# When the second mixing's weights are prepared: sums of half groups in blocks 2 to 6, second-layer parts in blocks 7 and 8, both kept in DRAM

## The chip, the core and the metric

The kernel runs on one core of a Trainium2 chip. The metric is the device time of one execution in microseconds (us), of which three runs of the kernel before are given. A core has five engines that work through their own queues in order: TensorE (PE, with its weight loads PEld), VectorE (DVE), ScalarE (ACT), GpSimd (POOL) and SyncE (SP), which here only issues transfers. ACT and POOL issue transfers too.

## The reference, cut to what matters

Three stages follow each other. Everything is float32; the weights come as float64 and are read as pairs of 32-bit words.

```
attention   (8 batches, 8 heads, 576 tokens, 64 wide): softmax of q over the width, of k over the tokens,
            kv = k_s^T v, out = q_s kv
first mixing   u  = x + (relu(x^T w_tok1) w_tok2)^T
               y  = u + relu(u w_ch1) w_ch2              512 -> 1536 -> 512
second mixing  xn = (y - mean) / sqrt(var + 1e-6) * g_ln
               out = y + relu(xn w2_ch1) w2_ch2          512 -> 2048 -> 512
```

## The kernel before, in words

Each float32 operand of a product is split into a high part (rounded by a copy to fp32r) and a low part (the rest), and three of the four partial products are made (`PASSES`). ACT makes the high part, POOL or DVE the low one. A weight in float64 is first turned into float32 bits: ACT rescales the upper word (`rebias`, L113), DVE makes three integer operations (L119, L126, L132), and then the two parts follow.

The first mixing runs over 4608 tokens in blocks of 512 tokens, numbered 0 to 8. A block makes 12 steps f; in each, `L1` makes 12 matmuls into `ph`, ACT and DVE take relu and split it into `h` (L155, L156), and `L2` makes 12 matmuls of the `h` of two steps earlier. In blocks 1 to 6 the attention of the next batch is made between these: a block has four units, and the function `Unit.start` sets on which tick (four ticks to a step) each unit's pieces are emitted. For the change it matters that a unit passes through all engines: DVE takes maxima `kmx`, `qm` and `kmd`, POOL subtracts (`qt` L486, `kt` L501), ACT takes exponentials, DVE sums `qs` (L518 to L520), POOL normalises `qt` (L521) and makes the low part of `qn` (L150, L530), PE multiplies `pk` and `pg`. At step 1 of a block the result of the block before is taken out of PSUM (`finish`: DVE `yT`, L745, then four POOL additions, L748) and turned back by PE (`py`, L659, in `y_store`).

The second mixing multiplies by w2_ch1 with seven products in place of eight for a 2 x 2 split (the sums S1 to S4 of weight quarters and the like sums of activations), over 6 slabs of 768 tokens and 8 groups of weights: 48 turns q, each with seven products `pp` (L1207) and the second layer of the turn before (`token_chunk`, L1245). `gather` on DVE and ACT takes each product out of one of two PSUM banks, so product i+2 waits for the gather of product i.

Before, `combine_all` decodes w2_ch1, makes the sums and splits them during blocks 7 and 8, and stores them in `wc_dram`; the turns load them from there (`ring_load`). The second-layer weights w2_ch2 (16 chunks of 128 rows) are loaded, decoded and split in place by `w2_jobs`: two chunks in block 8, two in turn 0 and twelve in turns 1 to about 6, a few operations after each product (`work`). There they share DVE, ACT and POOL with the gathers, the means and roots of the last block (`Root`, L775 to L789) and the normalisation of the next slab (`hat`, L1088, on POOL).

The order on each engine is the order in which the code emits; nothing reorders it. So an instruction that waits holds up all that stands behind it on its engine.

Of the kernel before, what the change touches and what calls it, by code (L numbers as in the profile page):

```python
# [8 lines left out]
F32 = mybir.dt.float32  # L9
# [15 lines left out]
def kernel(  # L25
# [66 lines left out]
    wc_dram = dram.tile([NP, P, 7, 512], F32, name="wc_dram")  # L92
# [586 lines left out]
    class Phase1:  # L679
# [51 lines left out]
        def finish(self):  # L731
# [9 lines left out]
            yT_t[self.j] = main.tile([P, KD, BLK], F32, tag="y", bufs=1, name="yT")  # L741
            yT, u = yT_t[self.j], u_t[self.j]
            for dd in range(KD):
                x = self.part[dd // 2][:, dd % 2] if self.f0 else u[:, 0, dd].bitcast(F32)
                nc.vector.tensor_tensor(out=yT[:, dd], in0=self.acc[dd], in1=x, op=ALU.add)  # L745
            def add(c):
# [14 lines left out]
    class Root:  # L761
# [5 lines left out]
        def start(self, at):  # L767
            for n, fn in zip((0, 2, 8, 11), (self.root, self.rstd, self.turn, self.store)):
                later(at + n, fn)
# [52 lines left out]
    SUMS = (1, 3, 4, 5)  # L822

    class Combine:


        def __init__(self, g):
            self.g = g

        def load(self):  # L830
            self.st = []
            for i in range(2):
                st = stage(512)
                a = w2_ch1[2 * i * P:2 * (i + 1) * P, 4 * self.g * P:4 * (self.g + 1) * P]
                nc.sync.dma_start(
                    out=st.rearrange("p (k f) t -> p k (f t)", k=2),
                    in_=a.rearrange("(k p) f -> p k f", p=P),
                )
                self.st.append(st)

        def decoding(self):

            both = [decode(st, None, None, None) for st in self.st]
            ops = [b[0] for b in both]
            for b in both:
                ops += [lambda b=b: [b[n]() for n in (1, 2, 3)], nop, nop]
            raw = [
                st[:, :, 0].bitcast(F32).rearrange("p (k f) -> p k f", k=2) for st in self.st
            ]
            self.a = {(f, k): raw[k][:, :, f * P:(f + 1) * P] for f in range(2) for k in range(2)}  # L850
            box = {}

            def add(o, x, y, op):
                def fn():
                    if o == 1:
                        self.s = w2p[0].tile([P, 4, 2, P], F32, tag="xc", bufs=7, name="wsum")
                    s = self.s
                    v = {"S1": s[:, 1], "S2": s[:, 0], "S3": s[:, 2], "S4": s[:, 3]}
                    pick = lambda n: v[n] if n in v else self.a[n]
                    nc.vector.tensor_tensor(out=s[:, o], in0=pick(x), in1=pick(y), op=op)  # L860
                return fn

            A11, A12, A21, A22 = (0, 0), (0, 1), (1, 0), (1, 1)
            ops += [
                add(1, A21, A22, ALU.add), add(0, "S1", A11, ALU.subtract),
                add(2, A11, A21, ALU.subtract), add(3, A12, "S2", ALU.subtract),
            ]
            return ops

        def splitting(self):  # L870
            s, a, box = self.s, self.a, {}
            A11, A12, A22 = a[0, 0], a[0, 1], a[1, 1]
            ops = []

            def tile_of(i):
                n = 0 if i < 3 else 3 if i < 5 else 5
                m = 3 if n == 0 else 2
                if n not in box:
                    box[n] = w2p[0].tile([P, m, 2, 2, P], F32R, tag="xc", bufs=7, name="wc")
                return box[n], i - n  # L880

            def part(x, i, n=1):
                def hi():
                    t, k = tile_of(i)
                    o = t[:, k:k + n, 0] if n > 1 else t[:, k, 0]
                    nc.scalar.activation(out=o, in_=x, func=AF.Copy)

                def lo():
                    t, k = tile_of(i)
                    o, h = (t[:, k:k + n, y] if n > 1 else t[:, k, y] for y in (1, 0))  # L890
                    nc.gpsimd.tensor_tensor(out=o, in0=x, in1=h.bitcast(F32), op=ALU.subtract)  # L891

                return [hi, lo]

            def store(n, m):
                def fn():
                    nc.sync.dma_start(
                        out=wc_dram[self.g, :, n:n + m],
                        in_=box[n].rearrange("p i x k f -> p i (x k f)").bitcast(F32),
                    )  # L900
                return fn

            ops += part(A11, 0) + part(A12, 2) + part(A22, 6)
            ops += part(s[:, 0], 1) + [store(0, 3)]
            ops += part(s[:, 1:3], 3, 2) + [store(3, 2)]
            ops += part(s[:, 3], 5) + [store(5, 2)]
            return ops

    w2p = []
    nop = lambda: None  # L910

    with tc.manual_schedule():
# [75 lines left out]
        jobs = []  # L988

        def work(n):  # L990
            for _ in range(n):
                if jobs:
                    jobs.pop(0)()

        def combine_all():

            cs = [Combine(g) for g in range(NP)]

            def expand(g):

                d = cs[g].decoding() if g < NP else []
                f = cs[g - 1].splitting() if g else []
                if 0 < g < NP - 1:
                    f.insert(6, cs[g + 1].load)
                ops = []
                while f or d[:-4]:
                    if f:
                        ops.append(f.pop(0))
                    if len(d) > 4:
                        ops.append(d.pop(0))  # L1010
                ops += d
                if g < NP:
                    ops.append(lambda: expand(g + 1))
                jobs[0:0] = ops

            jobs.extend([cs[0].load, cs[1].load] + [nop] * 20 + [lambda: expand(0)])

        def w2_jobs(chunks, stages, depth, ts=None, gap=12):

            st = {}  # L1020

            def load(n):
                g, i = n // 2, n % 2
                if i == 0:
                    wb2[g] = main.tile([P, 2, 2, DM], F32R, tag="w", bufs=NF1, name="w")
                st[n] = stages(n)
                nc.sync.dma_start(
                    out=st[n].rearrange("p d t -> p (d t)"), in_=w2_ch2[n * P:(n + 1) * P, :]
                )

            def go(n):
                ops = decode(
                    st[n], lambda x: x, wb2[n // 2][:, 0, n % 2], wb2[n // 2][:, 1, n % 2],
                    ts and ts[n % 2],
                )
                if not ts:
                    ops = [ops[0], lambda x=ops: [x[k]() for k in (1, 2, 3)], nop, ops[4]]
                jobs[0:0] = ops

            out = [lambda n=n: load(n) for n in chunks[:depth]] + [nop] * gap  # L1040
            for k, n in enumerate(chunks):
                out.append(lambda n=n: go(n))
                if k + depth < len(chunks):
                    m = chunks[k + depth]
                    out.append(lambda m=m: load(m))
            return out
# [4 lines left out]
        def ring_tile(i, x):  # L1051
            m = 4 if x == 0 else 3
            ring[i, x] = main.tile([P, m, 2, 2, P], F32R, tag="w", bufs=NF1, name="wr")

        def ring_load(q, x):
            n, m = ((0, 4), (4, 3))[x]
            nc.sync.dma_start(
                out=ring[q % 2, x].rearrange("p i x k f -> p i (x k f)").bitcast(F32),
                in_=wc_dram[q % NP, :, n:n + m],
            )  # L1060
# [44 lines left out]
        for o, f in steps:  # L1105
            if o.j == 1 and f == NF1 - 2:
                for hp in range(NHP):
                    Unit(2 * NHP + hp).start(OFF + 1 + hp * GAP)
                later(7, part.load_part)
            if f == 0:  # L1110
# [3 lines left out]
                elif o.j == B - 1:  # L1114
                    att.release()
                    w2pool = tc.alloc_tile_pool(name="w2pool", bufs=1, reuse_waits="tile")
                    w2p.append(w2pool)
                    bufs[:] = [
                        w2pool.tile([P, 512, 2], U32, tag="s3", name="stage3"),
                        w2pool.tile([P, 512, 2], U32, tag="xc", bufs=7, name="stage4"),  # L1120
                    ]
                    extra[:] = [-1, -1, 0, 1]
# [64 lines left out]
        while jobs:  # L1187
            work(1)
# [231 lines left out]
```

## Time and profile before

| quantity | value |
|---|---|
| median of three runs | 1648.15 us (1647.58 to 1649.58) |
| the profiled execution's own time | 1647.23 us |
| its span in the trace | 1645.5 us |
| PE busy | 1595.0 us, 97% |
| DVE, ACT, POOL busy | 819.1, 492.0, 498.5 us |
| mean granted clock of TensorE | 0.992 |

The busy times are sums over stages of different kind; what matters is where PE stands idle and what ends its wait. The span is cut into slices or stretches for that, and in a stretch the instructions are read in order of time.

### The profile page before, as it was taken

To read this page: it belongs to the slowest core of one execution; us is meant where nothing else is said; L and a number is where in the kernel's file an instruction comes from. 1 tells how busy PE (TensorE), PEld (TensorE's weight loads), DVE (VectorE), ACT (ScalarE), POOL (GpSimd) and SP (SyncE) were. 2 spreads that over 40 slices of the span, in tenths; PEclk is the share of its full clock that TensorE was granted. 3 is DMA by queue.
4 is the path that set the end of the run, shared out by engine and by line. 5 is a ranking of instruction groups with operands and counts; after the bars stand their busy time and mean duration, and the time that the engine had idled before them with its cause. 6 is when DMAs were issued, how large, how long until landed. Compare 5 with 4: busy or idle time off the path is not lost.

```text
span 1645.5 us, 21697 instructions
## 1 busy us (share of the span) xinstructions
PE 1595.0 (97%) x8241; PEld 1395.8 (85%) x8241; DVE 819.1 (50%) x1555; ACT 492.0 (30%) x1018; POOL 498.5 (30%) x412
## 2 busy tenths in 40 slices
PE   5999999999999999999998799999999999999998
PEld 4888888888888888888777688988989889889897
DVE  7776535444443534447857765335325335335233
ACT  5663333323232323324432222212222222122111
POOL 5744622232331424214662430310310310311001
PEclk8999999999999999999999899999999999999999
DMA  8542313112131313138766646445445544544341
GB/s 220 145 161 80 117 43 95 50 46 81 47 95 29 95 44 86 38 103 311 271 238 228 200 133 217 147 148 181 156 147 172 174 147 154 176 163 147 116 173 39
DMA packets 154398, 222.58 MB, mean 135 GB/s; under 512 B 97918, under 2 KB 114102, under 8 KB 146102
## 3 DMA queue, kind: packets, MB, share of 16 engines
q1 hardware_dynamic: 145750, 202.02, 38.6%
q10 hardware_dynamic: 5600, 9.73, 1.6%
q0 software_dynamic: 2944, 9.44, 1.6%
q8 instruction: 65, 1.06, 0.3%
q14 instruction: 39, 0.32, 0.1%
HBM read 174.98 MB, written 46.17 MB: 134 GB/s over the span
## 4 chain that ended last, share of the span: by engine, by line
PE 83%; DVE 5%; DMA 4%; POOL 3%; issue 2%; ACT 2%; SPq 1%; POOLq 0%; ACTq 0%; DVEq 0%
PE pp L1207 19%; PE ph L707 16%; PE acc L724 15%; PE acc L1245 15%; PE acca L1245 7%; PE pu L629 4%; PE pg L568 3%; PE pk L538 2%; DMA yb<-in_moe_w_ch 2%; PE pq L589 1%; PE py L659 1%; POOL wc L891 1%; PE pq L614 1%; DMA xs<-mr_dram 1%; DVE sd L119 1%
## 5 line engine op out<-in xcount | busy, mean ns | idle before, releaser
L1207 PE MATMUL pp<-xc,wr 128*128 128x384 f32 x2016 | 398.2, 340 | 16.2 <-DVE sc L1220 12.0
L1207 PEld LDWEIGHTS pp<-xc,wr 128*128 128x128 f32 x2016 | 361.1, 189 | 39.7 <-DVE sc L1220 15.4
L707 PE MATMUL ph<-u,w 128*128 128x512 f32 x1296 | 326.3, 397 | 2.9 <-DVE h L156 2.8
L724 PE MATMUL acc<-h,w 128*128 128x512 f32 x1296 | 323.9, 395 | 0.0
L707 PEld LDWEIGHTS ph<-u,w 128*128 128x128 f32 x1296 | 238.0, 189 | 50.7 <-DVE h L156 3.3
L724 PEld LDWEIGHTS acc<-h,w 128*128 128x128 f32 x1296 | 237.2, 188 | 47.3
L1245 PE MATMUL acc<-w,hh 128*128 128x512 f32 x648 | 180.5, 393 | 0.0
L1245 PE MATMUL acc<-w,h 128*128 128x512 f32 x501 | 145.5, 398 | 0.4 <-DVE h L156 0.4
L1245 PEld LDWEIGHTS acc<-w,hh 128*128 128x128 f32 x648 | 121.6, 188 | 26.6
L156 DVE SCALAR_TENSOR_TENSOR h<-ph,h 128x512 fp32r<-128x512 f32 x108 | 74.1, 687 | 138.1 <-ACT h L155 137.9
L1088 POOL TENSOR_TENSOR xs<-xs 128x768 f32<-128x768 f32 x48 | 90.3, 1911 | 128.3 <-DMA xs<-mr_dram 128.3
L1261 POOL DMA_DIRECT2D out<-yb x32 | 17.7, 553 | 365.2 <-DVE yb L1257 365.2
L155 ACT ACTIVATE hh<-sc 128x384 fp32r<-128x384 f32 x96 | 50.5, 526 | 249.8 <-DVE sc L1220 247.3
L155 ACT ACTIVATE h<-ph 128x512 fp32r<-128x512 f32 x108 | 64.2, 595 | 169.0 <-PE ph L707 168.5
L1245 PE MATMUL acca<-w,hh 128*128 128x512 f32 x432 | 114.2, 391 | 0.0
L1220 DVE TENSOR_TENSOR sc<-su,pp 128x384 f32<-128x384 f32 x144 | 79.5, 552 | 61.5 <-PE pp L1207 60.7
L1245 PEld LDWEIGHTS acc<-w,h 128*128 128x128 f32 x501 | 93.9, 190 | 13.5 <-DVE h L156 1.3
L1220 DVE TENSOR_TENSOR su<-su,pp 128x384 f32<-128x384 f32 x96 | 53.1, 553 | 102.4 <-PE pp L1207 102.2
L486 POOL TENSOR_TENSOR qt<-rawq,qm 128x640 f32<-128x640 f32 x24 | 30.3, 1261 | 228.0 <-PE pt L480 130.5
L156 DVE SCALAR_TENSOR_TENSOR hh<-sc,hh 128x384 fp32r<-128x384 f32 x96 | 63.4, 661 | 63.0 <-ACT hh L155 63.0
L1245 PEld LDWEIGHTS acca<-w,hh 128*128 128x128 f32 x432 | 80.5, 188 | 14.0
L629 PE MATMUL pu<-w,hs 128*128 128x288 f32 x384 | 61.8, 295 | 0.2 <-POOL w L150 0.2
(196 smaller groups left out, 1933.1 us busy)
## 6 DMA issues: line engine op xcount, KB each, us to landing
wr<-wc_dram SPq DMA_DIRECT2D x48, 1024.0 KB, 5.2
wr<-wc_dram SPq DMA_DIRECT2D x48, 768.0 KB, 4.5
st<-in_moe_w_ch SPq DMA_DIRECT2D x19, 512.0 KB, 4.8
yT_dram<-yT SPq DMA_DIRECT2D x9, 1024.0 KB, 5.0
vt<-in_v SPq DMA_DIRECT2D x64, 128.0 KB, 3.1
y_dram<-yn ACTq DMA_DIRECT2D x32, 256.0 KB, 2.6
wc_dram<-wc SPq DMA_DIRECT2D x16, 512.0 KB, 4.0
out<-yb POOLq DMA_DIRECT2D x32, 256.0 KB, 3.0
```

Of the source, the lines that this page charges most:

```text
L155: nc.scalar.activation(out=hi, in_=x, func=AF.Relu)
L156: nc.vector.scalar_tensor_tensor(out=lo, in0=x, scalar=0.0, in1=hi.bitcast(F32), op0=ALU.max, op1=ALU.subtract)
L486: nc.gpsimd.tensor_tensor(out=self.qt, in0=self.qr.rearrange("p h c d -> p c h d"), in1=self.qm.unsqueeze(3).to_broadcast([P, NC + 1, 2, D ...
L538: nc.tensor.matmul(out=pk[:, 0:2 * D + 2], lhsT=self.kt[:, c], rhs=vts[self.n % 2 if self.early else 0][:, c, :], start=(c == 0), stop=(c ...
L568: nc.tensor.matmul(out=pg[:, 0:T], lhsT=self.qn[:, x, c], rhs=w1[:, y, c, :], start=(n == 0), stop=(n == len(terms) - 1),)
L629: nc.tensor.matmul(out=pu[:, 0:HN], lhsT=l, rhs=r, start=(n == 0), stop=(n == len(terms) - 1))
L707: nc.tensor.matmul(out=ps, lhsT=w[:, x, kk, fo:fo + P], rhs=u[:, y, kk], start=(n == 0), stop=(n == 3 * KD - 1),)
L724: nc.tensor.matmul(out=self.acc[dd], lhsT=w[:, x, f % 2, dd * P:(dd + 1) * P], rhs=h[:, y], start=(f == self.f0 and n == 0), stop=(f == se ...
L1088: nc.gpsimd.tensor_tensor(out=y, in0=y, in1=m, op=(ALU.subtract, ALU.mult)[op])
L1207: nc.tensor.matmul(out=bank[(BANK[i] + q) % 2][:, 0:HT], lhsT=r[:, x, kk], rhs=xc[i][:, y, kk], start=(n == 0 and not add), stop=(n == 5), ...
L1220: nc.vector.tensor_tensor(out=o, in0=x, in1=y, op=ALU.add)
L1245: nc.tensor.matmul(out=acc[c], lhsT=h[:, x, m * P:(m + 1) * P], rhs=wb2[p][:, y, f], start=(p == 0 and n == 0), stop=(p == NP - 1 and n == 5),
```

## The change

`Sums` takes the place of `Combine`. It works on a half group (both 128-row quarters of one half of K, 512 KB in float64) in a cycle of eight jobs, one job after each `L1` and one after each `L2`, from block 2, step 3 on: `first` and `bits` and the first line of `add` decode within the staging tile, `add` makes the four sums there, `out` makes the parts of a half, `store` writes them, and with the second store the next half group is loaded. Loads and stores are issued by ACT. The staging tile and the tile of parts are the two buffers of tag "s"; the second `out` writes the buffer that the first `store` reads. Sixteen half groups at eight jobs and 24 jobs a block end in block 7, step 5; steps 0, 4 and 8 of a block have `first` and `bits`, steps 1, 5 and 9 have `add` and `out`, and so on.

`Rows` takes the place of `w2_jobs`: a chunk of 128 rows of w2_ch2 a step in block 7, two a step in block 8 up to step 3; ACT rescales, DVE makes three operations, ACT and POOL split, POOL issues the store to `we_dram`. `load_w2` loads a pair of chunks by SP: three in block 8, the rest in turns 0, 1 and 3.

Further: `finish` of the last block may do two of its four additions at a time, `Root` emits its last two pieces later (14 and 18 ticks in place of 8 and 11), and the weight tiles have another order of their dimensions.

```diff
-    wc_dram = dram.tile([NP, P, 7, 512], F32, name="wc_dram")
+    wc_dram = dram.tile([NP, P, 2, 2, 4, P], F32, name="wc_dram")
+    wd_dram = dram.tile([NP, P, 2, 2, 3, P], F32, name="wd_dram")
+    we_dram = dram.tile([NP, P, 2, 2, DM], F32, name="we_dram")
...
-    class Combine:
...
+    def two_parts(x, o):
+        nc.scalar.activation(out=o[:, 0], in_=x, func=AF.Copy)
+        nc.gpsimd.tensor_tensor(out=o[:, 1], in0=x, in1=o[:, 0].bitcast(F32), op=ALU.subtract)
...
+    class Sums:
...
+            for n in range(2 * NP):
+                self.jobs += [
+                    self.first, self.bits, self.add, lambda n=n: self.out(n, 0), self.store,
+                    lambda n=n: self.out(n, 1),
+                    lambda n=n: (self.store(), self.load(n + 1)), nop,
+                ]
...
+        def add(self):
+            w0, w1 = self.st[:, :, 0], self.st[:, :, 1]
+            nc.vector.tensor_tensor(out=w0, in0=w0, in1=w1, op=ALU.bitwise_or)
...
+        def out(self, n, h):
+            o = main.tile([P, 2, 4, P], F32R, tag="s", bufs=2, name="so")
...
+        def store(self):
+            nc.scalar.dma_start(out=self.done[0], in_=self.done[1].bitcast(F32))
+
+    class Rows:
...
+        def parts(self, n):
+            o = self.tile()[:, 0:1024].bitcast(F32R).rearrange("p (x d) -> p x d", x=2)
+            two_parts(self.view(n)[:, :, 0].bitcast(F32), o)
+            nc.gpsimd.dma_start(out=we_dram[n // 2, :, n % 2], in_=o.bitcast(F32))
...
+        def mix_weights(o, f, late):
+            if (2, 3) <= (o.j, f) < (B, 0):
+                mix_sums.run()
+            if mix_rows and o.j < B - late or o.j == B and f < 4:
+                mix_rows[0].run()
...
-        at(0, 3, lambda: pend[0][0].L2(*pend[0][1:], nop, range(2)))
+        at(0, 3, lambda: [pend[0][0].L2(*pend[0][1:], nop, range(2)), lastp.finish(range(2))])
...
-            jobs.extend(w2_jobs([*range(4, NF2)], flat64, 3, ts, 0))
```

Two places show the new order. The first is DVE at steps 0 to 2 of a block with attention (block 4); `kmx`, `qm`, `kmd` and `qs` are those of the block's first unit, `h` the relu of a step, `yT` the result of the block before. Before:

```order
L457 TENSOR_REDUCE kmx<-rawk 128x128
L463 TENSOR_REDUCE qm<-rawq 128x10
L482 TENSOR_REDUCE kmd<-pt 128x1
L156 SCALAR_TENSOR_TENSOR h<-ph_4205,h 128x512
L518 TENSOR_REDUCE qs<-qt 128x10
L519 TENSOR_SCALAR qs<-qs 128x10
L520 RECIPROCAL qs<-qs 128x10
L745 TENSOR_TENSOR yT<-acc_3462,u 128x512
```

The same stretch of DVE in the changed kernel; `st` is the staging tile:

```order
L459 TENSOR_REDUCE kmx<-rawk 128x128
L880 TENSOR_SCALAR st<-st 128x512
L465 TENSOR_REDUCE qm<-rawq 128x10
L886 SCALAR_TENSOR_TENSOR st<-st 128x512
L889 TENSOR_SCALAR st<-st 128x512
L484 TENSOR_REDUCE kmd<-pt 128x1
L158 SCALAR_TENSOR_TENSOR h<-ph_4318,h 128x512
L896 TENSOR_TENSOR st<-st 128x512
L905 TENSOR_TENSOR st<-st 128x128 x4
L520 TENSOR_REDUCE qs<-qt 128x10
L521 TENSOR_SCALAR qs<-qs 128x10
L522 RECIPROCAL qs<-qs 128x10
```

Three operations of 512 columns now stand ahead of `kmd`, and one of 512 and four of 128 columns between `h` and `qs`. On POOL a low part of the sums (`so`) stands between the normalised `qt` and the block result `yT`, ahead of the unit's `qn`. Before:

```order
L501 TENSOR_TENSOR kt<-rawk,kb 128x640
L521 TENSOR_TENSOR qt<-qt,qs 128x640
L748 TENSOR_TENSOR yT<-yT,u 128x4x128
L150 TENSOR_TENSOR qn<-qt,qn 128x512
L530 TENSOR_TENSOR qn<-qt,qn 64x128
```

And POOL in the changed kernel at the same place:

```order
L503 TENSOR_TENSOR kt<-rawk,kb 128x640
L523 TENSOR_TENSOR qt<-qt,qs 128x640
L843 TENSOR_TENSOR so<-st,so 128x512
L754 TENSOR_TENSOR yT<-yT,u 128x4x128
L152 TENSOR_TENSOR qn<-qt,qn 128x512
L532 TENSOR_TENSOR qn<-qt,qn 64x128
```

One operation has been put in. The second place is DVE in turn 2 of the second mixing, from the gather of its second product on (`su`, `sc` and `hh` are gathers, `sd` and `yb` the decode of w2_ch2, `ve` begins the roots). Before:

```order
L1220 TENSOR_TENSOR su<-su,pp 128x384
L775 TENSOR_SCALAR ve<-mr 128x8
L111 TENSOR_SCALAR yb<-yb 128x512
L119 TENSOR_SCALAR sd<-yb 128x512
L1220 TENSOR_TENSOR sc<-su,pp 128x384
L156 SCALAR_TENSOR_TENSOR hh<-sc,hh 128x384
L126 SCALAR_TENSOR_TENSOR sd<-yb,sd 128x512
L132 SCALAR_TENSOR_TENSOR sd<-yb,sd 128x512
```

And in the changed kernel:

```order
L1218 TENSOR_TENSOR su<-su,pp 128x384
L781 TENSOR_SCALAR ve<-mr 128x8
L1218 TENSOR_TENSOR sc<-su,pp 128x384
L158 SCALAR_TENSOR_TENSOR hh<-sc,hh 128x384
L1218 TENSOR_TENSOR sc<-su,pp 128x384
L158 SCALAR_TENSOR_TENSOR h_8020<-sc,h_8020 128x384
L789 RECIPROCAL mr<-mr 128x2x4
L790 TENSOR_TENSOR r_8370<-mr 128x8
L791 TENSOR_TENSOR r_8370<-r_8370,ve 128x8
```

The decode operations between the gathers are gone; the roots stand where they stood.

## Rows read from the trace of the kernel before

**Rows 1.** Slices of the span (busy tenths); a stretch: PE, PEld, DVE, ACT, POOL busy, clock.
```profile
PE   5999999999999999999998799999999999999998
...
900.00:1000.00 100.00, 89.15 (x413) 77.78 (x413) 66.63 (x96) 25.91 (x49) 35.95 (x22) 0.95 0.52 176
```

**Rows 2.** Groups by line, 780 to 975 us: busy, mean ns | idle before, releaser.
```profile
L1207 PE MATMUL pp<-xc,wr 128*128 128x384 f32 x258 | 55.8, 358 | 16.2 <-DVE sc L1220 12.0 <-DVE hw L156 2.0 <-DVE h L156 1.2
...
L707 PE MATMUL ph<-u,w 128*128 128x512 f32 x144 | 36.9, 405 | 2.8 <-DVE h L156 2.8
...
L659 PE MATMUL py<-ident,yT 128*128 128x128 f32 x32 | 4.8, 273 | 1.2 <-DVE st L132 1.2
```

**Rows 3.** PE in order of time: start, length, [idle before, releaser].
```profile
736.23 0.63 PE L659 MATMUL py<-ident,yT 128*128 128x128 f32 x4 [0.82 <-DVE st L132]
...
841.77 2.88 PE L724 MATMUL acc<-h,w 128*128 128x512 f32 x12
847.48 4.61 PE L707 MATMUL ph<-u,w 128*128 128x512 f32 x12 [2.84 <-DVE h L156]
...
912.78 2.29 PE L1207 MATMUL pp<-xc,wr 128*128 128x384 f32 x6 [1.68 <-DVE sc L1220]
...
919.44 2.29 PE L1207 MATMUL pp<-xc,wr 128*128 128x384 f32 x6 [2.61 <-DVE sc L1220]
...
924.77 1.21 PE L1207 MATMUL pp<-xc,wr 128*128 128x384 f32 x6
...
939.69 2.29 PE L1207 MATMUL pp<-xc,wr 128*128 128x384 f32 x6 [2.91 <-DVE sc L1220]
```

**Rows 4.** DVE in order of time, turns 2 to 4.
```profile
914.84 1.57 DVE L784 TENSOR_TENSOR r<-mr 128x8 f32<-128x8 f32 x1
916.44 1.73 DVE L785 TENSOR_TENSOR r<-r,ve 128x8 f32<-128x8 f32 x1
...
938.22 0.95 DVE L111 TENSOR_SCALAR yb<-yb 128x512 f32<-128x512 f32 x1 [2.98 <-DMA yb<-in_moe_w_ch]
```

**Rows 5.** DVE and POOL in order of time, block 8 and turn 2.
```profile
805.70 0.43 DVE L860 TENSOR_TENSOR wsum<-st 128x256 f32<-128x256 f32 x1
...
816.75 4.02 POOL L1088 TENSOR_TENSOR xs<-xs 128x768 f32<-128x768 f32 x2
817.13 1.95 DVE L860 TENSOR_TENSOR wsum<-wsum,stage 128x256 f32<-128x256 f32 x1
...
910.85 0.68 DVE L126 SCALAR_TENSOR_TENSOR sd<-yb,sd 128x512 uint32<-128x512 uint32 x1
```

**Rows 6.** A block with attention, steps 1 and 2, in order of time.
```profile
347.83 0.69 DVE L156 SCALAR_TENSOR_TENSOR h<-ph,h 128x512 fp32r<-128x512 f32 x1 [2.96 <-ACT h L155]
...
348.05 1.59 POOL L501 TENSOR_TENSOR kt<-rawk,kb 128x640 f32<-128x640 f32 x1 [1.89 <-ACT kb L497]
348.63 0.82 DVE L518 TENSOR_REDUCE qs<-qt 128x10 f32<-128x640 f32 x1
...
349.83 2.42 DVE L745 TENSOR_TENSOR yT<-acc,u 128x512 f32<-128x512 f32 x4
350.06 1.26 POOL L521 TENSOR_TENSOR qt<-qt,qs 128x640 f32<-128x640 f32 x1 [0.43 <-DVE qs L520]
...
352.34 1.27 POOL L748 TENSOR_TENSOR yT<-yT,u 128x512 f32<-128x512 f32 x1 [1.01 <-DVE yT L745]
...
354.10 1.30 POOL L150 TENSOR_TENSOR qn<-qt,qn 128x512 fp32r<-128x512 f32 x1 [0.49 <-ACT qn L148]
...
355.48 0.46 POOL L530 TENSOR_TENSOR qn<-qt,qn 64x128 fp32r<-64x128 f32 x1
...
356.43 1.81 PE L568 MATMUL pg<-w,qn 128*128 128x256 f32 x14
```

**Rows 7.** Stores, KB each, median us to landing; blocks 2 to 6, then 730 to 860 us.
```profile
yT_dram<-yT SPq DMA_DIRECT2D x5, 1024.0 KB, 5.0
...
wc_dram<-wc SPq DMA_DIRECT2D x16, 512.0 KB, 4.0
```

More of the change, by code (lines that the diff above doesn't have):

```diff
@@ L729, in L2, with finish @@
                     )
-        def finish(self):
+        def finish(self, dds=range(KD)):
             if self.f1 < NF1:
@@ L767, in start @@
         def start(self, at):
-            for n, fn in zip((0, 2, 8, 11), (self.root, self.rstd, self.turn, self.store)):
+            for n, fn in zip((0, 2, 14, 18), (self.root, self.rstd, self.turn, self.store)):
                 later(at + n, fn)
@@ L820, in runs @@
         return out
-    SUMS = (1, 3, 4, 5)
-    class Combine:
[L827 to L907, printed above, removed]
@@ new lines, with __init__, tile, load @@
+    class Rows:
+        def __init__(self, pool):
+            self.pool, self.st, self.n = pool, [], 0
+        def tile(self):
+            return self.pool.tile([P, 6 * P * 2], U32, tag="xc", bufs=7, name="xr")
+        def load(self, n):
+            if n < NF2:
+                x = self.tile()
+                self.st.append(x)
+                nc.sync.dma_start(out=x[:, 0:1024], in_=w2_ch2[n * P:(n + 1) * P, :])
+        def run(self):
+            n = self.n
+            self.n += 1
+            if n == 0:
+                for i in range(3):
+                    self.load(i)
+            if 0 <= n - 4 < NF2:
+                self.parts(n - 4)
+                self.load(n - 1)
+            if 0 <= n - 2 < NF2:
+                rebias(self.view(n - 2))
+            if 0 <= n - 3 < NF2:
+                st = self.view(n - 3)
+                single(st[:, :, 0], st[:, :, 1], self.st[n - 3][:, 1024:1536])
+        def view(self, n):
+            return self.st[n][:, 0:1024].rearrange("p (d t) -> p d t", t=2)
+        def parts(self, n):
+            o = self.tile()[:, 0:1024].bitcast(F32R).rearrange("p (x d) -> p x d", x=2)
+            two_parts(self.view(n)[:, :, 0].bitcast(F32), o)
+            nc.gpsimd.dma_start(out=we_dram[n // 2, :, n % 2], in_=o.bitcast(F32))
@@ L986, in do_L2 @@
                 o.finish()
[L988 to L1046, printed above, removed]
+        mix_sums, mix_rows = Sums(), []
@@ L1179 @@
             loads.pump(7 if now[0] < RUSH else 3)
-            work(7)
+            mix_weights(o, f, 1)
             pend.append((o, f, h))
@@ L1184 @@
                 loads.pump(4)
-                work(7)
+                mix_weights(o, f, 0)
                 tick()
-        while jobs:
-            work(1)
+        assert not mix_sums.jobs and mix_rows[0].n > NF2 + 3
         while ticks:
@@ L1285, in last_rows @@
             do_L2(nop, range(2, KD))
-            tmp["add"] = lastp.finish()
+            tmp["add"] = lastp.finish(range(2, KD))
             yn_t[B] = xs[0]
@@ L1328 @@
         at(1, 1, take_over)
+        for n in range(3, NP):
+            at((0, 0, 0, 1, 3)[n - 3], (4, 5, 6, 0, 1)[n - 3], lambda n=n: load_w2(n))
         at(1, 3, more_acc)
```

113 lines of the change are left out of this document (86 added, 27 removed).

## The prediction

> **What bounds the kernel now.** I read the 40 slices of the span first. PE is busy for 90% or more in all of them but the first, the last, and the 22nd and 23rd, which are 864 to 946 us; in the 100 us from 900 us it is busy for 89.15 us at a granted clock of 0.95 [rows 1]. So PE sets the pace nearly everywhere, in the attention blocks too, and time is to be had only where it waits: around the change of stages, 730 to 960 us. The groups by line of that stretch give the waits: 16.2 us before the products, nearly all for a DVE gather or relu, 2.8 us before `ph` and 1.2 us before `py` [rows 2]. With the 0.82 us before an earlier `py` [rows 3] that is 21.0 us. Then PE in order of time: after the long waits it runs at half clock for a while. Twelve matmuls of 512 columns took 4.61 us behind a wait of 2.84 us, where they take 2.88; six products took 2.29 us, where they take 1.21, behind three waits [rows 3]. That is 1.73 + 3 x 1.08 = 5.0 us more. In all 26.0 us are lost in this stretch.
>
> **What the change removes.** The waits for `py` name a DVE decode operation, the third of w2_ch1's, which holds one of the two PSUM buffers that `py` needs; the new decode stays in SBUF, so 2.0 us go. The wait of 2.84 us and its 1.73 us of half clock stand in step 11 of block 8, where ACT and DVE work off two chunks of w2_ch2 ahead of the relu; nothing of that is left there, and the small waits behind it go with it. In turns 0 to 5 the decode stands between the gathers; the wait of 2.91 us is a DVE operation that waited 2.98 us for a chunk to land, with a gather behind it [rows 3, 4]. After the change no decode stands in the turns, and the weights come by eight loads that SP issues at least a turn ahead of their use.
>
> One wait stays. The gather before 919.44 us came late behind the roots, whose two tiny additions took 1.57 and 1.73 us beside the normalisation on POOL [rows 4]; both stay in turn 2. I keep its 2.61 us and its 1.08 us of half clock [rows 3]. So 26.0 - 3.7 = 22.3 us go. At best the roots fall clear of POOL and all 26.0 go.
>
> **What it adds where PE is full.** In blocks 2 to 7 sixteen half groups put work on DVE, ACT and POOL. As a sum it fits: DVE about 3.4 us a half group (one or two operations of 0.68 us [rows 5], four of 128 columns, two simple ones), a half group lasting four steps, some 31 us. What costs is the order. Two jobs a step and 24 a block put the same job at the same step of every block, and at steps 1 and 2 of a block it meets the first unit and `finish` together, on a path that has little to spare: POOL ends `qn` at 355.94 us and PE starts `pg` at 356.43 [rows 6].
>
> Worked out on this block: DVE is through with `h` at 348.52 us. Next stands the OR of two SBUF operands (0.68 us), while POOL has been at `kt` since 348.05 us, until 349.64 [rows 6]. What that does is shown by the sums of before: an addition of two SBUF operands took 0.43 us alone and 1.95 us when it started 0.4 us after a POOL operation of some 2 us [rows 5]. So I let the OR wait for `kt`: it ends at 350.3. Four additions of half the columns of that 0.43 us one, each behind the one before: between 0.2 and 0.43 us each, I take 0.3, so 351.5. The three `qs` operations took 1.2 us (348.63 to 349.83), so 352.7; POOL's `qt` 1.26, 354.1; then the new low part, 512 columns like `qn`'s, 1.30, 355.4; `yT` 1.27, 356.7; `qn` 1.30 and 0.46, 358.5 [rows 6]. With hops `pg` starts at some 358.6, 2.2 us late. The other way round, DVE's four `yT` additions (2.42 us) end at 355.1 and don't set it. This happens in blocks 3, 4, 5 and 6: 4 x 2.2 = 8.8 us. The bounds: if the OR doesn't wait and an addition takes 0.2 us, DVE is done 1.5 us earlier and `pg` is 0.7 us late; if the three operations ahead of `kmd` get caught by POOL's `qt` as well, `pb` and all behind it come 0.9 us later, 3.1 us. So 2.8 to 12.4 us, and I stay by 8.8, since the addition of 1.95 us is the nearest row.
>
> The Trainium skill has the rule for this (SBUF — State Buffer, "Who interferes with whom"): a DVE instruction with two SBUF inputs and a GpSimd instruction that reads SBUF block each other fully, and the one that comes second waits to the other's end. The 1.95 us agree, and by it a block costs the 2.2 us; without it, by the lone durations, it would be 0.7 to 1.1 us.
>
> Elsewhere in blocks 2 to 6: at step 9 the low part stands ahead of the fourth unit's `qn`, which I work out to end about when `pg` wants it; at steps 2, 6 and 10 ACT waits for the landing of its own first store before it makes the second half's parts, since both use one buffer, and behind that wait stand a `gs`, a `kt` exponential or a relu that PE wants. A store of 512 KB landed in 4.0 us in the busy stretch, one of 1024 KB in 5.0 in these blocks [rows 7]; with 4.0 the three places come out with 0.1 to 1 us to spare. I take 0.5 us a block, 2.3 us for four and a half blocks; from nothing to 6.
>
> In block 8, steps 0 to 3, seven chunks meet `finish` and the statistics on DVE: by the prices above some 21 us of work in 22 us, before any waiting for POOL. A relu may come some 6 us late before PE stands. I take 1.5 us, from nothing to 4; as cover goes the two relus and the two-step lag between `L1` and `L2`. The POOL stores cost POOL alone, off the path until the normalisation at step 4.
>
> **Sum.** -22.3 + 8.8 + 2.3 + 1.5 = -9.7 us against the profiled execution's 1647.23, so 1637.5. The median of the runs lies 0.9 us higher, so 1638.4: I forecast 1638 us.
>
> **Rivals.**
>
> *The blocks swallow it.* The OR finds POOL free, the other places have their slack: the blocks cost 2.8 us and block 8 nothing. 1648.15 - 22.3 + 2.8 = 1629 us. For it: DVE, ACT and POOL have much idle time in these blocks. Against it: `pg` has half a microsecond and POOL is inside `kt` just when DVE comes [rows 6].
>
> *The turns don't get clean.* The waits are partly the roots, the normalisation and the loads, which stay, and the decode was only the last to be seen. If a third of the 22.3 us stays, 15 us go and 12.6 come: 1646 us, no change. For it: the long `r` operations [rows 4]. Against it: of the four long waits three have decode operations right before the late gather, and DVE is busy for 66.63 of 100 us there [rows 1].
>
> *ACT stands for its own stores.* It decides from the landing time. Each microsecond over 4.0 is paid at steps 2 and 6 of four and a half blocks, nine times; at 5.1 us the whole 9.7 us are eaten, at 6 it costs 18 us: 1656 us, slower. Against it: 1024 KB took 5.0 us in these blocks [rows 7]; for it: the wait is certain and stands on the engine that every relu needs.
>
> **How the numbers follow.** Within 0.2% of 1648.15, that is 1644.9 to 1651.4 us, a measurement can't tell it from no change. The forecast has 0.50, with a range of its own from 1632 to 1643; the blocks that swallow it 0.22; the turns that stay 0.16; ACT's stores 0.12. Faster gets nearly all of the first two and a little of the third, 0.73; no change the rest of the third and a little of the others, 0.16; slower most of the last, 0.11. For eight in ten I take 1626 to 1650: it holds the first three cases and the edge of the last.
>
> **What would show it.** Right: no wait of PE over 1 us between 840 us and turn 2, one of some 2 to 3 us in turn 2 behind the roots; in blocks 3 to 6 one wait before `pg` of about 2 us each, released by POOL `qn`, and `L896` over 1.5 us long where `kt` runs. Wrong: `pg` without a wait (the second case), waits before the products in turns 1 to 5 (the third), `gs` or `kt` on ACT released by a DMA with PE waiting behind (the fourth). What would make it wrong beyond these is a half clock behind the new waits, which I left out, since single waits under 2 us in the turns were not followed by it: the 0.82 us of rows 3 cost nothing more.

## The result, and the profile after

The changed kernel took 1626.73 us in the median of four runs (1625.88 to 1628.29); the kernel before, on the same chip, 1647.87 us. The ratio is 0.9871, 95% interval 0.9854 to 0.9888: 21 us less, where 10 were forecast. The direction was right; the size lies at the low edge of the range, and the terms for the attention blocks were together 9 us too high. One execution of the run with the roots later, below, took 2252.59 us at a granted clock of 0.66 where its other four took 1621.19 to 1623.56, and is left out of the median given there.

The slices of the page after have no dip left between the first and the last, where [rows 1] showed one in the 22nd and 23rd:

```profile
PE   5999999999999999999999999999999999999998
```

The same stretch as in [rows 1] (PE, PEld, DVE, ACT, POOL busy, clock):

```profile
900.00:1000.00 100.00, 97.15 (x485) 87.37 (x484) 46.82 (x75) 25.00 (x47) 23.61 (x17) 1.00 0.46 158
```

PE gains 8.0 us in these 100, and DVE is busy 19.8 us less (the work in this stretch stands some 10 to 20 us further on than before). All waits of PE behind 720 us (who waited for whom: us in total, times, longest):

```profile
PE py L661 <- POOL yT L754: 3.2, 1, 3.2
PE pp L1205 <- DVE sc L1218: 2.9, 1, 2.9
PE acc L726 <- ACT xr L842: 0.2, 1, 0.2
```

So of the 21.0 us in [rows 2, 3] the one wait behind the roots is left (the two additions of the roots took 1.58 and 1.72 us here), and a new one for `py` has come. The new one and what PE does behind it, in order of time (start, length, [idle before, releaser]):

```profile
809.95 1.11 PE L661 MATMUL py<-ident,yT 128*128 128x128 f32 x4 [3.19 <-POOL yT L754]
810.72 2.71 PE L709 MATMUL ph<-u,w 128*128 128x512 f32 x6
...
814.63 0.60 PE L661 MATMUL py<-ident,yT 128*128 128x128 f32 x4
```

The stretch right behind the wait (PE, PEld, DVE, ACT, POOL busy, granted clock):

```profile
810.00:813.00 3.00, 3.00 (x10) 2.52 (x10) 2.97 (x2) 0.00 (x0) 2.70 (x3) 0.50 0.55 153
```

Four transposes take 1.11 us where they take 0.60 a little later, and six matmuls of 512 columns 2.71 where six take 1.53. This is half clock, and the row shows it: the granted clock is 0.50, which is 1.2 of 2.4 GHz. Over the three long rows of six products in [rows 3] it is 0.50 as well.

PE has the same matmuls in the same order in both kernels but for one transpose of `pm`. So the start of one and the same matmul can be compared, and the difference (after less before) shows where time comes and goes:

| the same matmul, before and after (us) | after less before | in between |
|---|---|---|
| `pb` of the first unit, 17.48 and 17.05 | -0.43 | |
| `pq`, block 6, 640.34 and 642.01 | +1.67 | blocks 1 to 6: +2.1 |
| `py`, 736.23 and 737.00; `py`, 800.37 and 800.24 | +0.77; -0.13 | two old `py` waits gone: -1.8 |
| `acc`, 808.63 and 813.26 | +4.63 | new `py` wait, half clock: +4.8 |
| first `pp`, 852.33 and 851.84 | -0.49 | wait of step 11 gone: -5.1 |
| last matmuls, 1638.49 and 1616.79 | -21.70 | turns 0 to 5: -21.2 |

The last transfers took 0.9 us longer after, which makes 20.8 in the spans, 1645.5 and 1624.7 us. Against the sum of the prediction:

| term | forecast | measured |
|---|---|---|
| lost before and gone, the roots kept | -22.3 | -28.1 (1.8 + 5.1 + 21.2) |
| blocks with attention | +8.8 + 2.3 | +2.1 |
| block 8 | +1.5 | +4.8 |

Steps 1 and 2 of the block of [rows 6], after, in order of time (all engines; rows left out):

```profile
347.60 1.58 POOL L503 TENSOR_TENSOR kt<-rawk,kb 128x640 f32<-128x640 f32 x1 [1.25 <-ACT kb L499]
348.00 1.73 DVE L896 TENSOR_TENSOR st<-st 128x512 uint32<-128x512 uint32 x1
...
349.76 1.15 DVE L905 TENSOR_TENSOR st<-st 128x128 f32<-128x128 f32 x4
...
350.83 0.81 DVE L520 TENSOR_REDUCE qs<-qt 128x10 f32<-128x640 f32 x1
...
352.24 1.26 POOL L523 TENSOR_TENSOR qt<-qt,qs 128x640 f32<-128x640 f32 x1 [3.06 <-DVE qs L522]
...
353.46 1.33 POOL L843 TENSOR_TENSOR so<-st,so 128x512 fp32r<-128x512 f32 x1
353.54 0.74 ACT L150 ACTIVATE qn<-qt 128x640 fp32r<-128x640 f32 x1 [0.16 <-POOL qt L523]
...
354.74 1.31 POOL L754 TENSOR_TENSOR yT<-yT,u 128x512 f32<-128x512 f32 x1
...
355.99 1.32 POOL L152 TENSOR_TENSOR qn<-qt,qn 128x512 fp32r<-128x512 f32 x1
...
356.40 1.99 PE L570 MATMUL pg<-w,qn 128*128 128x256 f32 x14
...
357.39 0.45 POOL L532 TENSOR_TENSOR qn<-qt,qn 64x128 fp32r<-64x128 f32 x1
```

The delay came nearly as forecast: the OR stood for `kt` (1.73 us), the four additions took 0.29 us each, and POOL ends `qn` at 357.84 us, 1.90 us later than in [rows 6], where 2.6 were worked out (POOL began `kt` 0.45 us sooner here). But `pg` starts at 356.40 without a wait, 0.9 us before POOL has ended the low part (357.31) and 1.4 before the tail; it only takes 1.99 us where it took 1.81.

The stores of the sums landed faster than the 4.0 us assumed from [rows 7] (KB each, median us to landing, 150 to 720 us):

```profile
wc_dram<-so ACTq DMA_DIRECT2D x14, 512.0 KB, 2.6
```

### The profile page after: what moved, and what is told of

Same layout as the page of the kernel before. It is cut to its first block, busy times and chain, and to the rows that moved or that the text cites. A ratio compares the mean times of both kernels' runs of the same rounds, so it can differ in the third digit from the quotient of the medians.

```text
span 1624.7 us, 21829 instructions
## 1 busy us (share of the span) xinstructions
PE 1587.8 (98%) x8241; PEld 1393.0 (86%) x8241; DVE 820.1 (50%) x1589; ACT 503.3 (31%) x1032; POOL 507.5 (31%) x428
## 4 chain that ended last, share of the span: by engine, by line
PE 91%; DVE 3%; POOL 2%; issue 2%; ACT 1%; DMA 1%; SPq 0%; POOLq 0%; DVEq 0%; ACTq 0%
PE pp L1205 22%; PE ph L709 17%; PE acc L726 17%; PE acc L1243 16%; PE acca L1243 8%; PE pu L631 4%; PE pg L570 3%; PE pk L540 2%; PE py L661 1%; PE pq L591 1%; PE pq L616 1%; POOL yT L754 0%; DMA stages<-in_moe_w_tok 0%; DVE st L889 0%; DVE kmx L459 0%
## 5 line engine op out<-in xcount | busy, mean ns | idle before, releaser
L1205 PE MATMUL pp<-xc,wr 128*128 128x384 f32 x2016 | 393.4, 338 | 2.9 <-DVE sc L1218 2.9
L1259 POOL DMA_DIRECT2D out<-yb x32 | 17.6, 550 | 375.9 <-DVE yb L1255 375.9
L158 DVE SCALAR_TENSOR_TENSOR hh<-sc,hh 128x384 fp32r<-128x384 f32 x96 | 59.3, 618 | 63.3 <-ACT hh L157 63.3
L843 POOL TENSOR_TENSOR so<-st,so 128x512 fp32r<-128x512 f32 (+2 forms) x48 | 39.8, 843 | 111.6 <-ACT so L842 102.8
```

Of the source, the lines that this page charges most:

```text
L158: nc.vector.scalar_tensor_tensor(out=lo, in0=x, scalar=0.0, in1=hi.bitcast(F32), op0=ALU.max, op1=ALU.subtract)
L843: nc.gpsimd.tensor_tensor(out=o[:, 1], in0=x, in1=o[:, 0].bitcast(F32), op=ALU.subtract)
L1205: nc.tensor.matmul(out=bank[(BANK[i] + q) % 2][:, 0:HT], lhsT=r[:, kk, x], rhs=xc[i][:, y, kk], start=(n == 0 and not add), stop=(n == 5), ...
```

## The experiments

Theory: `pg` wasn't late because its fourteen matmuls read the high part of `qn`, which ACT makes, eight times before they touch the low part. The rival: the lateness is made good behind `pg`. The changed kernel ran once more, as a base on the chip of the next three:

> The changed kernel once more, beside which the other runs of this series are read. Both theories: 1626.7 us, 0.987 of the kernel before.

It took 1626.98 us (ratio 0.9877, 0.9864 to 0.9891), as the first time.

### The low part read first

```diff
             terms = [(x, y, c) for x, y in PASSES for c in range(NC)] + [(0, 0, NC), (0, 1, NC)]
+            if not self.early:
+                terms = terms[3 * NC:] + terms[2 * NC:3 * NC] + terms[:2 * NC]
```

> The changed kernel with one line more: pg's fourteen matmuls read qn's tail and low part, which POOL makes, first, and the high part, which ACT makes, last; the sum is the same. Theory 'read order': in blocks 3 to 6 POOL ends qn of the first unit 1.44 us after pg starts (357.84 against 356.40 us), and PE doesn't stand because pg's first eight matmuls read the high part alone. With the low part first pg must wait for POOL: 1.44 and some 0.1 us for the hop, less the 0.18 us by which pg is longer now, in four blocks, 5.5 us; and 1.1 us for one unit of block 1, where POOL ends 1.0 us after pg's start too. 6.6 us more: 1633 us, with four waits of PE of about 1.5 us before pg, released by POOL. Rival 'taken up behind': the steps behind pg have room, and a late pg is made good before the block ends: not over 1628 us.

> The kernel before with the same line: the control. There POOL ends qn 0.49 us ahead of pg in these blocks, so the order costs nothing but the one unit of block 1, 1.1 us. Theory 'read order': 1649 us, no wait before pg in blocks 3 to 6. If this one grows by as much as the changed kernel does, the order of the matmuls costs by itself, and the comparison says nothing on POOL's lateness.

Measured: 1636.0 us (0.9928, 0.9916 to 0.9941), 9.0 us more than the changed kernel; the control 1647.91 beside 1647.49 us (1.0004, 0.9995 to 1.0012). PE's waits for `pg` in the changed kernel with this line, then one of them in PE's order of time:

```profile
PE pg L572 <- POOL qn L532: 6.1, 5, 1.3
```

```profile
359.56 1.86 PE L572 MATMUL pg<-w,qn 128*128 128x256 f32 x14 [1.28 <-POOL qn L532]
```

Five waits: 0.92 us in block 1, which the control has too, and four of 1.3 in blocks 3 to 6. Matched matmul by matmul with the changed kernel, it loses 6.4 us in the blocks, as forecast; most of the rest is lost behind the roots in turn 2, where its granted clock fell to 0.50. The theory holds: with the order of before, POOL's 1.9 us cost PE next to nothing; with the low part first the same lateness costs about what I had forecast, and in the kernel before, where POOL isn't late in blocks 3 to 6, the order is free there.

### The sums alone

In the changed kernel `Rows` and `load_w2` are replaced by the old `w2_jobs`, with the weight tiles' new order:

```diff
-                    mix_rows.append(Rows(w2pool))
...
-                if f in (8, 9, 10):
-                    later(4, lambda p=f - 8: load_w2(p))
+                if f == 7:
+                    jobs += w2_jobs([0, 1], lambda n: stage(512), 2)
...
+        at(0, 0, lambda: jobs.extend(w2_jobs([2, 3], flat64, 2, ts, 6)))
...
+            jobs.extend(w2_jobs([*range(4, NF2)], flat64, 3, ts, 0))
...
+                work(2 + (q > 0))
```

> Half of the change undone: the sums are made in blocks 2 to 6 as in the changed kernel, but the second layer's parts are made as in the kernel before, two chunks in block 8 and fourteen between the gathers of turns 0 to 6. Theory 'the decode in the turns': the waits of step 11 of block 8 (2.84 us and 1.73 us of half clock) and of turns 0 to 5 come back, 4.9 and some 21 us; the 5.0 us that the changed kernel loses in block 8 beside the stores of POOL go: 1626.7 + 4.9 + 21.2 - 5.0 = 1648 us, as long as the kernel before, so the half with the sums buys nothing by itself. Rival 'the loads': the turns became clean because the sums no longer share block 8 and the loads of turn 0 with the decode, and the decode alone fits between the gathers: 1627 to 1633 us.

Measured: 1638.82 us (0.995, 0.9934 to 0.9965), between the two. Matched with the changed kernel, it is 18.3 us slower from 866 us on (-5.3 to +13.0): the turns' waits are the decode of w2_ch2, as the prediction said, 3 us less of them than expected. But the wait of step 11 does not come back, though the same two chunks are decoded ahead of the same relu. The reason stands in ACT's rows of the same rescaling of the first chunk, in the kernel before and then in this run:

```profile
837.22 0.68 ACT L113 ACTIVATE st<-st 128x512 f32<-128x512 f32 x1 [5.53 <-DMA st<-in_moe_w_ch]
```

```profile
830.61 0.66 ACT L114 ACTIVATE st<-st 128x512 f32<-128x512 f32 x1
```

SP's rows for the load of these two chunks, in the same order; before, three stores of the sums stand right ahead of it:

```profile
828.46 2.98 SPq L897 DMA_DIRECT2D wc_dram<-wc  x3
831.53 2.25 SPq L1027 DMA_DIRECT2D st<-in_moe_w_ch  x2
```

```profile
816.86 0.89 SPq L1020 DMA_DIRECT2D st<-in_moe_w_ch  x2
```

Before, the load was issued at 831.53 us and ACT stood 5.53 us for the chunk to land, in a block whose queue and staging tiles the sums shared; here it was issued at 816.86 us, the chunk is there, ACT is through with both chunks at 837.64 us and not at 845.21, and the relu is in time. Whether the queue or the tiles held the load back before was not tried. So the expectation was wrong in that part: the wait at step 11 goes with the sums, not with the second layer's weights. The half with the sums is worth 8.7 us (1647.49 to 1638.82), the half with the second layer another 11.8 (to 1626.98), taken in this order and already less the 4.8 that it loses in block 8. The first half holds the small changes to `finish` and `Root` as well, which were not tried alone.

### The two waits that are left

```diff
-                    later(2 * c if self.j > 1 else 0, lambda c=c: add(c))
+                    later(2 * c if 1 < self.j < B - 1 else 0, lambda c=c: add(c))
```

> The changed kernel with block 7's four additions to yT on POOL issued together, ahead of the second layer's parts of block 8's steps, and not two steps apart. Theory 'behind the parts': PE waits 3.19 us for py (and then loses 0.51 and 1.08 us at half clock) because the third addition stands on POOL behind a low part of 1.42 us and a store's issue. Ahead of them it is done by 804 us, the wait goes, and the time falls by 4.8 us: 1622 us. Rival 'POOL is full there': the parts then come 5 us later and hold up the loads of w2_ch2 or the normalisation, and a wait of the same size stands elsewhere in block 8: 1626 us.

```diff
-        at(2, 3, root.root)
-        at(2, 5, root.rstd)
-        at(3, 0, root.scatter)
+        at(5, 3, root.root)
+        at(5, 5, root.rstd)
+        at(6, 0, root.scatter)
```

> The changed kernel with the roots of the last two blocks in turn 5 (steps 3 and 5, stored in turn 6), where POOL normalises nothing, and not in turn 2. Theory 'roots beside the normalisation': the two additions of 8 elements of 1.58 and 1.72 us take some 0.2 us each there, the gather of turn 2 is no longer behind them, and 2.85 us of waiting and 0.12 us behind it go: 1623.8 us. Rival 'the normalisation alone': the relu ahead of the roots takes 2.06 us beside it too, and the gather stays late by some 1.5 us: 1626 us.

> Both moves in one kernel: the additions at once, and the roots in turn 5. If both theories hold they add up, and PE has no wait over 0.7 us between 150 us and the end: 1626.7 - 4.8 - 3.0 = 1618.9 us. If one of the rivals holds, 1622 to 1624 us; if both, 1626 us.

The last run of these four has both moves, and the sums' jobs begin two steps later:

```diff
-            if (2, 3) <= (o.j, f) < (B, 0):
+            if (2, 5) <= (o.j, f) < (B, 0):
```

> Both moves, and the sums' jobs begin two steps later, so that in every block the OR and its additions fall at steps 3, 7 and 11 in place of 1, 5 and 9. Theory 'read order': the sums cost some 0.45 us a block in blocks 3 to 6 (pb 0.16 us late, pg 0.18 us longer, the rest in between), because POOL's low part comes late at steps 1 and 2 only; elsewhere the low part has more room, and up to 1.8 us go: 1617 to 1619 us. Rival 'it is the place after all': at the new steps the same work meets another unit's qn or a relu, and blocks 2 to 6 cost 2 to 9 us more: 1621 to 1628 us.

| run | median us | ratio to before, interval |
|---|---|---|
| additions at once | 1625.66 | 0.9874 (0.9861 to 0.9888) |
| roots later | 1622.92 | 0.9851 (0.9836 to 0.9866) |
| both | 1623.07 | 0.9851 (0.9838 to 0.9865) |
| both, sums two steps later | 1621.95 | 0.9847 (0.9834 to 0.9861) |

The roots behaved as expected; DVE in order of time with the roots in turn 5, the operations of [rows 4] and the gather behind them:

```profile
946.58 0.17 DVE L790 TENSOR_TENSOR r<-mr 128x8 f32<-128x8 f32 x1
946.78 0.17 DVE L791 TENSOR_TENSOR r<-r,ve 128x8 f32<-128x8 f32 x1
...
947.27 0.55 DVE L1218 TENSOR_TENSOR sc<-su,pp 128x384 f32<-128x384 f32 x1
```

0.17 us in place of 1.57 and 1.73, no wait of PE is left in the turns, and, matched with the changed kernel, 3.1 us go. The theory on the additions fell: PE's wait for `py` only changed its releaser, and with the roots already moved, the additions at once change nothing clear of noise (1623.07 beside 1622.92 us). With the additions at once, DVE, POOL, ACT and PE (one row of each engine's order of time):

```profile
797.16 5.79 DVE L834 SCALAR_TENSOR_TENSOR xr<-xr 128x512 uint32<-128x512 uint32 x1
```

```profile
797.39 5.01 POOL L754 TENSOR_TENSOR yT<-yT,u 128x512 f32<-128x512 f32 x4
```

```profile
803.72 0.67 ACT L842 ACTIVATE xr<-xr 128x512 fp32r<-128x512 f32 x1 [6.65 <-DVE xr L837]
...
808.23 0.58 ACT L669 ACTIVATE yn<-py 128x512 f32<-128x512 f32 x1
```

```profile
808.96 0.63 PE L661 MATMUL py<-ident,yT 128*128 128x128 f32 x4 [2.96 <-ACT yn L669]
```

A DVE operation of 0.69 us with two SBUF operands stands for all four additions, ACT stands 6.65 us for what follows it, and its copy of the first `py`, which frees the PSUM buffer for the third, comes at 808.23 us. That is the rule of the Trainium skill that the prediction cited (SBUF — State Buffer, "Who interferes with whom"); the trace agrees that the two shut each other out, but not on which of them waits: by the recorded starts DVE came 0.23 us first, and it is DVE that stands. Here DVE also didn't get in between four POOL instructions in a row; in the fastest version, below, it did. The half clock behind the wait didn't appear this time (0.63 us): matched with the changed kernel, 1.5 us are gained there, and 1.3 of them lost again behind the roots, where six products took 2.23 us in place of 1.33. With both moves the granted clock was 0.50 behind the wait for `py` again. The two steps' shift of the sums took the four waits of 0.16 us before `pb` away and is 1.1 us faster by the medians, inside both intervals. Matched with the run of both moves it gains 1.9 us, some 0.5 in each of blocks 3 to 6 and nothing elsewhere, the size that the theory of the read order named; but one profile of each is all there is for it.

### Taking the second layer's parts out of block 8

```diff
-            if mix_rows and o.j < B - late or o.j == B and f < 4:
+            if mix_rows and o.j == B - 1 and (not late or f > 3):
```

> The roots in turn 5, the sums two steps later (both as in the runs before), the additions two steps apart again as in the changed kernel, and the second layer's parts all made in block 7: one chunk a step in its steps 0 to 3, two from step 4 on, none in block 8. Theory 'DVE stands for the additions': in block 8 the two-input operations of DVE and POOL's additions to yT shut each other out (5.79 us for one beside four additions), and py waits by way of ACT or of POOL, whichever order they have; without the parts in block 8 there is nothing to meet, the wait of 3.0 to 3.2 us with its half clock goes, and the time is 1622.3 - 4.8 - 0.2 = 1617.3 us, with no wait over 0.7 us behind 150 us. Rival 'two a step is too much for DVE in block 7 as well': waits for relus of the same size come in block 7: 1622 us or more.

> The same with block 7's additions issued at once. Theory 'DVE stands for the additions': with no parts in block 8 their order is worth nothing, 1617.3 us as the run before. Rival 'the order counts': it differs by over 2 us.

Measured: 1632.54 us (0.9913, 0.99 to 0.9927) and 1633.11 us (0.9915, 0.9901 to 0.9929). Matched with the changed kernel, the first of them loses 17.6 us in block 7 and gains 5.3 in block 8. Block 8 is clean and the order of the additions is worth nothing, as the theory had it; but block 7 isn't clean. PE's waits in the first of the two, and one row of ACT there:

```profile
PE ph L709 <- DVE h L158: 11.7, 5, 4.7
```

```profile
766.07 0.65 ACT L847 ACTIVATE xr<-xr 128x512 f32<-128x512 f32 x1 [5.96 <-DMA xr<-in_moe_w_ch]
```

Two chunks a step outrun their loads: ACT stands 5.96 us for a chunk, with a relu behind it, and the sums still run in this block. The rival came, and dearer than it said.

### The price of ACT's wait for its stores

```diff
+    copies = dram.tile([3, 2 * NP, 2, P, 2, 4, P], F32, name="copies")
...
             nc.scalar.dma_start(out=self.done[0], in_=self.done[1].bitcast(F32))
+            m = self.done[1].shape[2]
+            for i in range(3):
+                nc.scalar.dma_start(
+                    out=copies[i, self.done[2], self.done[3], :, :, 0:m],
+                    in_=self.done[1].bitcast(F32),
+                )
```

> The changed kernel with every store of the sums issued four times on ACT, the copies to memory that nothing reads, so that the first half's buffer comes free late. The store of 512 KB lands in 2.6 us here, where 4.0 were assumed. The prediction's price: each microsecond over 4.0 is paid at nine places; with some 6.5 us to the last landing that is 22 us: 1649 us. Theory 'read order' widened: what ACT makes after the wait is wanted by PE later than I worked out, as with qn: under 1632 us, with ACT waiting for the copies some 6 us at ten places and PE for hardly any.

Measured: 1671.67 us (1.0155, 1.0135 to 1.0175), 45 us more than the changed kernel. ACT in order of time at steps 1 and 2 of the block shown above, then the largest of PE's waits:

```profile
357.35 0.34 ACTq L921 DMA_DIRECT2D wc_dram<-so  x1
357.73 2.52 ACTq L924 DMA_DIRECT2D copies<-so  x3
363.94 0.64 ACT L843 ACTIVATE so<-st 128x256 fp32r<-128x256 f32 x2 [6.34 <-DMA copies<-so]
364.49 0.36 ACT L576 ACTIVATE gs<-pg 128x256 f32<-128x256 f32 x1
```

```profile
PE py L662 <- ACT gs L576: 14.3, 4, 3.9
PE pk L541 <- ACT kt L517: 8.1, 6, 2.5
```

The last copy lands 6.6 us after the first store's issue, and `gs` and `kt` stand behind it, two of the three that the prediction named (the third, a relu, makes PE wait 5.3 us in all). The widened theory fell clearly, and the prediction's own price (22 us) was too low by half. From 150 to 800 us PE is idle for 27.3 us, where it is idle for 1.5 in the changed kernel, and its mean granted clock is 0.98 in place of 1.00, so that half clock behind the waits adds to them. The copies also cost ACT 2.52 us of issuing at this place, and the queue their bytes; how much of the 45 us is due to these was not measured apart. The changed kernel doesn't meet this price because 512 KB land in 2.6 us, not because the place has endless room.

### The fastest version

Both moves, the sums two steps later, and the four `py` of block 7 at the steps of all other blocks:

```diff
-                later((5, 8, 12, 15)[c] if self.j < B - 1 else 5 + 2 * c, lambda c=c: y_store(self.j, c))
+                later((5, 8, 12, 15)[c], lambda c=c: y_store(self.j, c))
```

> The fastest version so far (roots in turn 5, sums two steps later, additions at once), and block 7's four turns of y (py) at the steps that every other block has them, 5, 8, 12 and 15, and not 5, 7, 9 and 11. Theory 'ACT behind DVE': the third py waits 3.0 us because ACT, standing for the DVE operation of 5.79 us, copies the first one's PSUM only at 808.23 us; a third py some 4 us later finds it free, and the wait goes with no other in its place: 1618.9 us. Rival 'the step is full': one of the relus or copies of block 8's first steps is late then, and 1 to 3 us of it stay: 1620 to 1622 us.

Measured: 1617.23 us (1616.99 to 1618.52; 0.9821, 0.9808 to 0.9834), 9.5 us less than the changed kernel. All of PE's waits behind 150 us:

```profile
PE acc L726 <- DVE yT L748: 1.0, 1, 1.0
PE pk L540 <- ACT kt L516: 0.6, 1, 0.6
```

The wait for `py` is gone, and one of 1.0 us for the additions of DVE has taken its place. It is faster than the theory said (1618.9 us), and the theory is not shown by it: the operation of 5.79 us, for which ACT was to stand, is gone as well. The same decode operations and the four additions in this run, DVE and then POOL in order of time:

```profile
796.57 0.69 DVE L834 SCALAR_TENSOR_TENSOR xr<-xr 128x512 uint32<-128x512 uint32 x1
797.30 1.71 DVE L837 SCALAR_TENSOR_TENSOR xr<-xr 128x512 uint32<-128x512 uint32 x1
...
800.48 1.67 DVE L834 SCALAR_TENSOR_TENSOR xr<-xr 128x512 uint32<-128x512 uint32 x1
802.18 1.66 DVE L837 SCALAR_TENSOR_TENSOR xr<-xr 128x512 uint32<-128x512 uint32 x1
```

```profile
797.14 6.15 POOL L754 TENSOR_TENSOR yT<-yT,u 128x512 f32<-128x512 f32 x4
```

The first operation was nearly through when POOL began, the next started 0.16 us behind POOL, and from there the two engines took turns: 1.66 to 1.71 us for each of these DVE operations, 6.15 us for the four additions in place of 5.01. So the 4.7 us of this step may come from the later `py` or from the other meeting of DVE and POOL; the runs don't tell these apart.

## Why the prediction was wrong in size, step by step

**What bounds the kernel, and what goes.** Right in kind: all gathers that were late behind a decode are in time, and one wait behind the roots stays, 2.85 us and 0.12 behind it (forecast 2.61 and 1.08). Mis-sized: 28.1 us went where 22.3 were forecast. The 5.0 us for half clock counted only the first group behind a wait. Three more groups stood behind it in the kernel before at 1.27 to 1.45 us for three matmuls that take 0.86, and every wait loses some more at its edges: six products behind a short wait take 1.32 us in place of 1.21, and in a full stretch the next row starts 0.16 us before the modelled end of the one before it. Matched matmul by matmul, 26.2 us go between 836 and 965 us: 16.5 are idle time, about what the forecast had, 6.2 are half clock, where it had 3.9, and 3.5 are these edges, which it left out. Its reason for leaving out half clock behind the new waits, that waits under 2 us were not followed by it, does not hold in its own rows either: the wait of 1.68 us in [rows 3] has 2.29 us behind it (another wait, of 2.35 us, stood shortly ahead of it). PE's busy time for the same matmuls bears it out: 1595.0 us before, 1587.8 after.

**The step that failed:** "With hops `pg` starts at some 358.6, 2.2 us late. ... This happens in blocks 3, 4, 5 and 6: 4 x 2.2 = 8.8 us." Everything up to POOL's end was right to 0.7 us. The last link was not: [rows 6] show POOL's `qn` ending 0.49 us before `pg` starts, and I took that for the whole of `pg`'s room. The row of `pg` has no bracket, so PE wasn't waiting there; and in the kernel before one `pg` in block 1 starts at 190.88 us while POOL ends that `qn`'s low part at 191.37:

```profile
190.07 1.30 POOL L150 TENSOR_TENSOR qn<-qt,qn 128x512 fp32r<-128x512 f32 x1
...
190.88 1.81 PE L568 MATMUL pg<-w,qn 128*128 128x256 f32 x14
```

The order of the matmuls in `tok1` gives the room: POOL's low part is first read by the ninth. The runs put 0.2 us per block in place of 2.2; where the low part is read first, they put 6.4 us in all, 1.1 of them in block 1. The rest of blocks 1 to 6 makes some 1.3 us (2.1 less four times 0.2), where 2.3 were forecast. Half of it is the start of the case that the prediction's upper bound named: an operation ahead of `kmd` is caught by POOL's `qt` (0.43 us alone), and `pb` waits in four blocks:

```profile
345.26 1.37 DVE L889 TENSOR_SCALAR st<-st 128x512 uint32<-128x512 uint32 x1
```

```profile
PE pb L495 <- DVE kmd L484: 0.7, 4, 0.2
```

**Block 8:** 4.8 us where 1.5 were forecast (nothing to 4). I looked to the relus; it is the third `py`, behind POOL's third addition, which the parts of w2_ch2 held up (and, with the additions at once, behind ACT, which stood for the same parts). The prediction let all of the `py` waits go with the decode's PSUM buffers; those went, and this one came.

**The wait of step 11** went, but for another reason than I gave: the late landing of the chunk, not the work on it. The run with the sums alone has the same work there, with the load issued earlier, and no wait.

**The rivals.** "The blocks swallow it" came nearest to the size, 1629 us, and the blocks did swallow their work, though not by its reason: the OR did not find POOL free. That it is only 2 us off is luck in part: it had 22.3 us gone and nothing for block 8, and 5.8 us more went while 4.8 came. "The turns don't get clean" is refuted by the waits. "ACT stands for its own stores": ACT does stand, 2.50 us at step 2 of the block shown, but the landing of 2.6 us leaves PE untouched; its price was shown to be real.

## What to carry to other kernels

A row that starts just after one of its inputs is ready shows neither that it waited nor how much room it has: look for the wait, and ask which instruction of the group is the first to read the late part. A long in-order group can be given room by reading first what is ready first. And before counting a wait as removed with its seeming cause, look at what that cause itself waited for: the decode at step 11 was late because its data were late.

## What the runs showed that was not expected

A DVE operation of 0.69 us with two SBUF operands took 5.79 us beside four POOL additions (5.01 us) that, by the trace, started 0.23 us after it. The two other runs with the additions at once beside these parts, and the `py` steps unchanged, show the same (5.82 and 5.80 us); where the DVE operation started 0.16 us behind POOL, in the fastest version, it stood for one addition alone. Half clock behind a wait could not be told from the wait's length. In the first profile of the changed kernel the gather behind the roots made PE wait 2.85 us, and six products then took 1.33 us; in the profile of its second series the same place shows a wait of 2.43 us and 2.29 us for the same six. After 3.19 us before `py` six matmuls took 2.71 us, after 2.96 us in the run with the additions at once 1.63.
